# Two more token tiles transposed by DMA, the x loads re-ordered around it, and W1 loaded from two queues

## Chip, cores, metric

One core of one Trainium2 chip. The metric is the device time of one execution in microseconds (us); a time is the median of several runs, and a comparison uses runs of the two kernels taken on the same chip in the same rounds. Ratios are the mean time of one kernel's fast runs over that of the other's of the same rounds, so they are not quite the ratio of the medians quoted. "KB" is 1024 bytes.

## The reference

A layer norm of x (2048 tokens, 640 features) feeds two branches that are summed onto x: linear attention with 32 heads, and an MLP with GELU. Only the MLP's first product concerns us.

```python
xn = _layernorm(x)
h  = gelu(einsum("bsd,df->bsf", xn, w1) + b1)        # d = 640, f = 1536
return x + attention(xn, wqkv, wo) + einsum("bsf,fd->bsd", h, w2) + b2
```

## The kernel before

The 2048 tokens are 16 tiles of 128. Each is normalised token-major (`xn_tm`, DVE) and must be transposed (`xnT`) before TensorE (PE) can multiply it by W1. Tiles 0 to 3 are transposed by PE into PSUM and copied out; tiles 4 to 15 by a transposing DMA on the SP queue. A wait is placed by the helper `Pl.ins` from the `reads` and `writes` of each operation. The SP queue works in program order: a transposing DMA that waits for its tile also holds all that stands behind it. A "unit" below is 128 of W1's columns times one, two or four tiles: 5 products, one for each 128 of the 640 features. The code is shortened to its order:

```python
dma_x(0, 1)                                              # SP: x0
dma_w("scalar", W1[:, 0:KA, 0:FW], ..., r_W1A)           # ACT: 2/5 of W1's first third
dma_x(1, 1)
dma_w("sync", W1[:, KA:DT, 0:FW], ..., r_W1[0])          # SP: its other 3/5
dma_w1(1); dma_x(2, 1); dma_w1(2); dma_x(3, 1)           # W1's other thirds, whole; x2, x3
dma_x(4, 2); dma_x(6, 2); dma_x(8, 4); dma_x(12, 4)      # all other x, before any transpose
# ... [cut]
h_first(0, [0, 1, 2, 3], r_xnTA, ...)      # tiles 0, 1 with W1's first third, 128 columns
h_first(1, [0, 1, 2, 3], r_xnTA1)
units(0, 2, JQ, 2 * JQ + 1)                # tiles 0+1, 256 columns, 5 products a unit
ln_stats(2); ln_norm(2); ln_stats(3)
xnT_copy(2, transp(2))                     # PE transpose of tile 2, DVE copy
units(0, 2, 2 * JQ + 1, JT)
ln_next(3)                                 # statistics of tile 4 around the norm of 3
units(2, 1, 0, 3)
xnT_copy(3, transp(3))                     # the same for tile 3
units(2, 1, 3, 6); ln_next(4); units(3, 1, 0, 6); units(2, 2, 6, JT)
for t in range(TD, NT):                    # TD = 4
    if t > TD: ln_next(t)
    # SP: dma_start_transpose(xnT tile t <- xn_tm tile t)
```

Of the kernel before, what the change touches and what calls it, by code (L numbers as in the profile page):

```python
# [7 lines left out]
P = 128  # L8
# [104 lines left out]
def bass_parallel_sum__linear_attn_block__dense_activation_gelu__prompt_kernel(  # L113
# [4 lines left out]
    NT = S // P  # L118
    CH = 4
    CW = CH * P  # L120
    NC = NT // CH
    DT = D // P
    JT = F // P
# [6 lines left out]
    Pl = Planner(nc)  # L130
    R_ = Pl.res
# [5 lines left out]
    with contextlib.ExitStack() as es:  # L137
# [5 lines left out]
        xn_tm = sb("xn_tm", [P, NT, D], BF16)  # L143
        xnTf = sb("xnT", [P, DT * S], BF16)
        xnT = xnTf[:].rearrange("p (k s) -> p k s", k=DT)
# [4 lines left out]
        W1 = W1f[:].rearrange("p (k f) -> p k f", k=DT)  # L150
        GTb = W1f[:, 0:DT * D].rearrange("p (k d) -> p k d", k=DT)
        KVT = W1f[:, DT * D:2 * DT * D].rearrange("p (k d) -> p k d", k=DT)
# [27 lines left out]
        B_ = [R_("bank%d" % i) for i in range(8)]  # L180
# [10 lines left out]
        def bank(b, lo=0, hi=512):  # L191
            return ps[:, b * 512 + lo: b * 512 + hi]
# [10 lines left out]
        r_xn = [R_("xn%d" % t) for t in range(NT)]  # L203
        r_xnT = [R_("xnT%d" % t) for t in range(NT)]
        NW1 = 3
        r_W1A = R_("W1_0A")
        r_W1 = [R_("W1_%d" % i) for i in range(NW1)]
        r_Wq, r_Wk, r_Wv, r_W2, r_Wo = R_("Wq"), R_("Wk"), R_("Wv"), R_("W2"), R_("Wo")
        r_b1tmp, r_b1c, r_b2 = R_("b1tmp"), R_("b1c"), R_("b2")
# [8 lines left out]
        r_GT = [R_("GT%d" % f) for f in range(DT)]  # L218
        r_KVT = R_("KVT")
# [8 lines left out]
        def dma_x(t, n):  # L228
            src = xv[t * P:(t + n) * P, :].rearrange("(t p) d -> p t d", p=P)
            Pl.ins("sync", lambda e: e.dma_start(x_in[:, t:t + n, :], src),  # L230
                   writes=r_x[t:t + n], dma=True)

        def dma_w(eng, dst, src, res):
            Pl.ins(eng, lambda e: e.dma_start(dst, src), writes=[res], dma=True)

        w1v = B_w1.rearrange("(k p) n -> p k n", p=P)
        wqv = A_wqkv.rearrange("(k p) n -> p k n", p=P)
        FW = F // NW1
        def dma_w1(i, eng="sync"):
            dma_w(eng, W1[:, :, i * FW:(i + 1) * FW], w1v[:, :, i * FW:(i + 1) * FW], r_W1[i])  # L240
        KA = 2
        dma_x(0, 1)
        dma_w("scalar", b1tmp[:], B_b1.rearrange("(a p) -> a p", p=P), r_b1tmp)
        dma_w("scalar", W1[:, 0:KA, 0:FW], w1v[:, 0:KA, 0:FW], r_W1A)
        dma_x(1, 1)
        dma_w("sync", W1[:, KA:DT, 0:FW], w1v[:, KA:DT, 0:FW], r_W1[0])
        dma_w1(1)
        dma_x(2, 1)
        dma_w1(2)
        dma_x(3, 1)  # L250
        dma_x(4, 2)
        dma_x(6, 2)
        for c in range(2, NC):
            dma_x(c * CH, CH)
        x_done = len(Pl.records["sync"])
        dma_w("sync", Wqkv[:, :, D:2 * D], wqv[:, :, D:2 * D], r_Wk)
        dma_w("sync", Wqkv[:, :, 0:D], wqv[:, :, 0:D], r_Wq)
# [5 lines left out]
        g = "gpsimd"  # L263
# [8 lines left out]
               reads=[r_ident], writes=[r_ident])  # L272

        mask_jobs = []
# [15 lines left out]
        def run_masks(n):  # L290
            for _ in range(min(n, len(mask_jobs))):
                mask_jobs.pop(0)()


        def filler(n):
            b = take(1)
            Pl.ins("tensor", [lambda e: e.matmul(bank(b), warm[:, 0:P], warm[:], start=True, stop=True)
                              for _ in range(n)], reads=[r_warm], writes=[B_[b]])
# [25 lines left out]
        def ln_stats(t):  # L324
            ln_half(t, 0)
            ln_half(t, 1)
            ln_aggr(t)

        def ln_norm(t):
            s = t % 4  # L330
            Pl.ins(v, lambda e: e.tensor_scalar(xn_tm[:, t, :], x_in[:, t, :], aggr[:, s, 0:1], rstd[:, s:s + 1],
                                                ALU.subtract, ALU.mult),
                   reads=[r_x[t], r_aggr[s], r_rstd[s]], writes=[r_xn[t]])

        def transp(t):
            b = take(1)
            pT = bank(b).bitcast(BF16)[:, 0:D]
            Pl.ins("tensor", [(lambda e, k=k: e.transpose(pT[:, k * P:(k + 1) * P],  # L338
                                                          xn_tm[:, t, k * P:(k + 1) * P], ident[:]))
                              for k in range(DT)],  # L340
                   reads=[r_xn[t], r_ident], writes=[B_[b]])
            return b

        def xnT_copy(t, b):
            pT = bank(b).bitcast(BF16)[:, 0:D]
            Pl.ins(v, lambda e: e.tensor_copy(xnT[:, :, t * P:(t + 1) * P],
                                              pT.rearrange("p (k q) -> p k q", k=DT)),
                   reads=[B_[b]], writes=[r_xnT[t]])

        def h_unit(t0, n, jb):  # L350
            b = take(1)
            w = n * P
            tok = slice(t0 * P, t0 * P + w)
            Pl.ins("tensor", [(lambda e, k=k: e.matmul(  # L354
                bank(b, 0, w), W1[:, k, jb * P:(jb + 1) * P], xnT[:, k, tok],
                start=(k == 0), stop=(k == DT - 1))) for k in range(DT)],
                reads=[r_W1[jb * P // FW]] + r_xnT[t0:t0 + n], writes=[B_[b]])
            Pl.ins("scalar", lambda e: e.activation(  # L358
                HG[:, jb, tok], bank(b, 0, w), ACT.Gelu_apprx_tanh, bias=b1c[:, jb:jb + 1]),
                reads=[B_[b], r_b1c], writes=[r_HG[t][jb] for t in range(t0, t0 + n)])  # L360
# [20 lines left out]
        def h_first(t, jbs, resA, between=None):  # L381
            bs = [take(1) for _ in jbs]
            tok = slice(t * P, (t + 1) * P)
            for (ks, res) in (((0, 1), resA), ((2, 3, 4), r_xnT[t])):
                for i, (jb, b) in enumerate(zip(jbs, bs)):
                    Pl.ins("tensor", [(lambda e, k=k, jb=jb, b=b: e.matmul(  # L386
                        bank(b, 0, P), W1[:, k, jb * P:(jb + 1) * P], xnT[:, k, tok],
                        start=(k == 0), stop=(k == DT - 1))) for k in ks],
                        reads=[r_W1A if res is resA else r_W1[jb * P // FW], res], writes=[B_[b]])
                    if between and res is not resA and i in between:  # L390
                        between[i]()
            for jb, b in zip(jbs, bs):
                Pl.ins("scalar", lambda e, jb=jb, b=b: e.activation(
                    HG[:, jb, tok], bank(b, 0, P), ACT.Gelu_apprx_tanh, bias=b1c[:, jb:jb + 1]),
                    reads=[B_[b], r_b1c], writes=[r_HG[t][jb]])
# [2 lines left out]
        r_xnA1, r_xnB1 = R_("xn1A"), R_("xn1B")  # L398
        Pl.ins("scalar", lambda e: e.activation(b1c[:, 0:1], warm[:, 0:1], ACT.Gelu_apprx_tanh),
               reads=[r_warm], writes=[r_b1c])  # L400
        filler(6)
        b1_step()
        filler(3)
# [6 lines left out]
        dA, sA, bA = transp_part(0, 0, 2, r_xnA)  # L410
# [12 lines left out]
                                          3: lambda: copy_part(2, DT, r_xnB1, r_xnT[1])})  # L423
        h_first(1, [0, 1, 2, 3], r_xnTA1)

        TD = 4
        late = Pl.records["sync"][x_done:]
        del Pl.records["sync"][x_done:]
        JQ = JT // NW1

        def units(t0, n, lo, hi):
            for jb in range(lo, hi):
                h_unit(t0, n, jb)

        def ln_next(t):
            if t + 1 < NT:
                ln_half(t + 1, 0)
            ln_norm(t)
            if t + 1 < NT:
                ln_half(t + 1, 1)  # L440
                ln_aggr(t + 1)

        units(0, 2, JQ, 2 * JQ + 1)
        ln_stats(2)
        ln_norm(2)
        ln_stats(3)
        xnT_copy(2, transp(2))
        units(0, 2, 2 * JQ + 1, JT)
        ln_next(3)
        units(2, 1, 0, 3)  # L450
        xnT_copy(3, transp(3))
        units(2, 1, 3, 6)
        ln_next(4)
        units(3, 1, 0, 6)
        units(2, 2, 6, JT)
        for t in range(TD, NT):
            if t > TD:
                ln_next(t)
            Pl.ins("sync", lambda e, t=t: e.dma_start_transpose(xnT[:, :, t * P:(t + 1) * P], xn_tm[:, t, :]),
                   reads=[r_xn[t]], writes=[r_xnT[t]], dma=True)  # L460
        Pl.records["sync"] += late
        run_masks(len(mask_jobs))
        units(4, 1, 0, 3)
        units(5, 1, 0, 3)
        units(4, 2, 3, JT)
# [20 lines left out]
        for t in range(NT):  # L486
            b = take(2)
# [7 lines left out]
            phi(pair(b), b, 2, PK[:, t, :], r_PK[t], [r_x[t]])  # L495


        Pl.ins(g, lambda e: e.memset(KVT, 0.0), writes=[r_KVT] + r_W1)


        def z_step():
# [25 lines left out]
        for f in range(DT):  # L527
            b = take(2)
            for t in range(NT):
                Pl.ins("tensor", [(lambda e, t=t, h=h, b=b, f=f: e.matmul(  # L530
                    bank(b + h, 0, HW), xn_tm[:, t, f * P:(f + 1) * P],
                    PK[:, t, h * HW:(h + 1) * HW], start=(t == 0), stop=(t == NT - 1))) for h in range(2)],
                    reads=[r_xn[t], r_PK[t]], writes=B_[b:b + 2])
            Pl.ins("scalar", lambda e, b=b, f=f: e.activation(halves(GTb[:, f, :]), pair(b), ACT.Copy),  # L534
                   reads=B_[b:b + 2], writes=[r_GT[f]] + r_W1)


        def q_chunk(c):
# [154 lines left out]
        for t in range(4, NT - 1):  # L693
            b = out_w2(t)
# [47 lines left out]
```

## Time and profile before

| | before |
|---|---|
| median, 6 runs | 207.86 us (207.61 to 208.02) |
| span of the profile | 206.3 us |
| PE busy | 98% |
| PE waits between 6 and 60 us | none listed |
| first third of W1 complete | 6.19 us |
| PE's first product of the attention branch | 59.84 us |

The profile gives each engine's busy time, a chain of work followed back from the last instruction, and who waited for whom. PE is busy throughout, so the time moves only with PE's own work and waits. Everything before 59.84 us is the part that the change touches, everything after it is the same in both kernels.

### The profile page before, as it was taken

Reading aid. Unit: us, or ns where it says so; the run is one execution under the profiler, and the core shown is the slowest. Engines: PE = TensorE matmul, PEld = TensorE weight load, DVE = VectorE, ACT = ScalarE, POOL = GpSimd, SP = SyncE. Lnnn points to the kernel's source line nnn. Section 1 sums busy time; section 2 is a strip of 40 time slices with the busy share of each in tenths; the row PEclk is TensorE's granted clock in tenths of the full one; section 3 lists DMA queues with packets and bytes.
Section 4 is the critical chain, followed back from the end, with each engine's and each line's share of the span. In section 5 each row is a group of like instructions: output and inputs, shape, how many; then the busy total and the mean of one; then the engine's idle time right before and its main releaser. Section 6 shows DMA issues by size and latency. Waiting matters only on the chain.

```text
span 206.3 us, 3886 instructions
## 1 busy us (share of the span) xinstructions
PE 202.4 (98%) x1562; PEld 139.7 (68%) x1562; DVE 114.1 (55%) x233; ACT 72.5 (35%) x136; POOL 21.4 (10%) x59
## 2 busy tenths in 40 slices
PE   7999999999999999999999999999999999999996
PEld 2799987444457777777756556777777777777775
DVE  4677677100007888999298887574863422522332
ACT  3589887666676455111153553400000000000000
POOL 3243434730031000000000000000000000000000
DMA  6993445499900000000300001932112111000102
GB/s 187 359 344 68 76 90 93 86 366 323 340 7 0 0 0 3 0 0 3 64 0 5 0 0 29 379 105 52 71 56 60 62 38 52 35 32 32 37 32 65
DMA packets 23210, 18.31 MB, mean 89 GB/s; under 512 B 10392, under 2 KB 23192, under 8 KB 23192
## 3 DMA queue, kind: packets, MB, share of 16 engines
q1 hardware_dynamic: 22896, 17.80, 29.0%
q10 hardware_dynamic: 296, 0.27, 0.4%
q8 instruction: 12, 0.20, 0.4%
q14 instruction: 6, 0.05, 0.1%
HBM read 12.62 MB, written 2.62 MB: 74 GB/s over the span
## 4 chain that ended last, share of the span: by engine, by line
PE 96%; DVE 1%; DMA 1%; issue 0%; DVEq 0%
PE ps L633 34%; PE ps L354 24%; PE ps L530 11%; PE ps L491 11%; PE ps L542 10%; PE ps L669 2%; PE ps L569 1%; PE ps L386 1%; DMA xPK<-in_A_x_dram 1%; DVE stats L310 1%; PE ps L551 1%; PE ps L580 1%; PE ps L375 0%; PE ps L338 0%; DVE xn_tm L368 0%
## 5 line engine op out<-in xcount | busy, mean ns | idle before, releaser
L633 PE MATMUL ps<-W,HG 128*128 128x320 bf16 x360 | 51.0, 299 | 0.0
L354 PE MATMUL ps<-xnT,W 128*128 128x256 bf16 (+2 forms) x385 | 50.5, 293 | 0.0
L633 PEld LDWEIGHTS ps<-W,HG 128*128 128x128 bf16 x360 | 35.1, 98 | 14.2 <-issue 0.4
L354 PEld LDWEIGHTS ps<-xnT,W 128*128 128x128 bf16 x385 | 33.9, 98 | 15.9
L358 ACT ACTIVATE HG<-ps,b1c 128x256 bf16<-128x256 f32 (+2 forms) x77 | 38.0, 516 | 12.7 <-PE ps L354 10.3
L652 DVE TENSOR_TENSOR out_sb<-ps,xnT 128x640 bf16<-128x640 f32 x15 | 12.4, 825 | 35.0 <-PE ps L633 34.8
L478 ACT ACTIVATE ek<-ps 128x512 bf16<-128x512 f32 (+1 forms) x36 | 23.2, 645 | 20.3 <-PE ps L542 10.6
L479 DVE TENSOR_SCALAR ek<-ek 128x512 bf16<-128x512 bf16 (+1 forms) x36 | 10.9, 304 | 25.9 <-ACT ek L478 24.8
L633 PE MATMUL ps<-Msb,PQ 128*128 128x320 bf16 x150 | 22.3, 299 | 0.0
L542 PE MATMUL ps<-xnT,Wqkv 128*128 128x512 bf16 x100 | 21.9, 379 | 0.0
L491 PE MATMUL ps<-Wqkv,xnT 128*128 128x320 bf16 x160 | 21.9, 299 | 0.0
L530 PE MATMUL ps<-xPK,xn_tm 128*128 128x320 bf16 x160 | 21.9, 299 | 0.0
L491 PEld LDWEIGHTS ps<-Wqkv,xnT 128*128 128x128 bf16 x160 | 15.7, 98 | 6.2
L530 PEld LDWEIGHTS ps<-xPK,xn_tm 128*128 128x128 bf16 x160 | 15.7, 98 | 6.1
L633 PEld LDWEIGHTS ps<-Msb,PQ 128*128 128x128 bf16 x150 | 14.7, 98 | 5.7
L542 PEld LDWEIGHTS ps<-xnT,Wqkv 128*128 128x128 bf16 x100 | 11.7, 117 | 9.5
L310 DVE BATCH_NORM_STATS2 stats<-xPK 128x6 f32<-128x320 bf16 x32 | 14.7, 470 | 2.5 <-DMA xPK<-in_A_x_dram 2.5
L481 DVE SCALAR_TENSOR_TENSOR PQ<-ps,ek 128x512 bf16<-128x512 f32 x20 | 13.8, 692 | 2.1
L481 DVE SCALAR_TENSOR_TENSOR xPK<-ps,ek 128x640 bf16<-128x640 f32 x16 | 13.2, 824 | 1.7
L517 DVE TENSOR_TENSOR Msb<-Msb,xPK 128x640 f32<-128x640 f32 x14 | 11.6, 825 | 0.5
L320 POOL TENSOR_TENSOR rstd<-aggr,mhalf 128x1 f32<-128x1 f32 x16 | 9.1, 569 | 15.7 <-DVE aggr L318 15.7
L534 ACT ACTIVATE W<-ps 128x640 bf16<-128x640 f32 x5 | 3.5, 704 | 18.2 <-PE ps L530 18.2
(62 smaller groups left out, 98.2 us busy)
## 6 DMA issues: line engine op xcount, KB each, us to landing
xnT<-in_A_x_dram SPq DMA_DIRECT2D x4, 640.0 KB, 6.4
Wqkv<-in_A_wqkv_dram SPq DMA_DIRECT2D x3, 800.0 KB, 6.9
out_dram<-out_sb SPq DMA_DIRECT2D x15, 160.0 KB, 1.8
W<-in_B_w_dram SPq DMA_DIRECT2D x1, 1920.0 KB, 15.0
W<-in_B_w_dram SPq DMA_DIRECT2D x2, 640.0 KB, 6.7
xPK<-in_A_x_dram SPq DMA_DIRECT2D x2, 640.0 KB, 9.7
Wo<-in_A_wo_dram SPq DMA_DIRECT2D x1, 800.0 KB, 10.4
xPK<-in_A_x_dram SPq DMA_DIRECT2D x4, 160.0 KB, 4.4
```

The costliest lines, as they stand in the source:

```text
L310: Pl.ins(v, lambda e: e.bn_stats(stats[:, s, 6 * h:6 * h + 6], x_in[:, t, h * HW:(h + 1) * HW]), reads=[r_x[t]], writes=[r_stats[s][h]])
L354: Pl.ins("tensor", [(lambda e, k=k: e.matmul(bank(b, 0, w), W1[:, k, jb * P:(jb + 1) * P], xnT[:, k, tok], start=(k == 0), stop=(k == DT - ...
L358: Pl.ins("scalar", lambda e: e.activation(HG[:, jb, tok], bank(b, 0, w), ACT.Gelu_apprx_tanh, bias=b1c[:, jb:jb + 1]), reads=[B_[b], r_b1c ...
L478: Pl.ins("scalar", lambda e: e.activation(e2, src, ACT.Exp), reads=br, writes=[r_ek[s]])
L479: Pl.ins(v, lambda e: e.tensor_scalar(et, et, 1.0, 1e-6, ALU.min, ALU.add), reads=[r_ek[s]], writes=[r_ek[s]])
L481: Pl.ins(v, lambda e: e.scalar_tensor_tensor(out=d2, in0=src, scalar=0.0, in1=e2, op0=ALU.max, op1=ALU.add), reads=br + [r_ek[s]], writes= ...
L491: fns.append(lambda e, k=k, h=h, b=b, t=t: e.matmul(bank(b + h, 0, HW), xnT[:, k, t * P:(t + 1) * P], Wqkv[:, k, D + h * HW:D + (h + 1) * ...
L517: Pl.ins(v, lambda e, t=t: e.tensor_tensor(out=zsum, in0=zsum, in1=PK[:, t, :], op=ALU.add), reads=[r_PK[t], r_zsum], writes=[r_zsum])
L530: Pl.ins("tensor", [(lambda e, t=t, h=h, b=b, f=f: e.matmul(bank(b + h, 0, HW), xn_tm[:, t, f * P:(f + 1) * P], PK[:, t, h * HW:(h + 1) * ...
L542: Pl.ins("tensor", [(lambda e, k=k, j=j, b=b: e.matmul(bank(b), Wqkv[:, k, j:D:DT], xnT[:, k, cc], start=(k == 0), stop=(k == DT - 1))) fo ...
L633: return lambda e: e.matmul(bank(b + h, 0, HW), l, r[:, h * HW:(h + 1) * HW], start=(i == 0), stop=(i == JT + DT - 1))
L652: Pl.ins(v, lambda e: e.tensor_tensor(out=halves(out_sb[:, s, :]), in0=pair(b), in1=halves(x_res[:, t, :]), op=ALU.add), reads=B_[b:b + 2] ...
```

## The change

Intent: take 10 transposing products (and two DVE copies) from PE, the busiest engine, and give them to DMA engines that are idle most of the time. To make tiles 2 and 3 early enough, x2 and x3 are loaded ahead of W1's later thirds, W1's two later thirds are split over SP's and ACT's queue as the first already is, and x6 to x15 move behind the new transposes.

```diff
+        def dma_w1(i):    # SP: 3/5 of a third of W1
+            dma_w("sync", W1[:, KA:DT, i * FW:(i + 1) * FW], ..., r_W1[i])
+        def dma_w1a(i):   # ACT: the other 2/5
+            dma_w("scalar", W1[:, 0:KA, i * FW:(i + 1) * FW], ..., r_W1A[i])
         dma_x(1, 1)
-        dma_w("sync", W1[:, KA:DT, 0:FW], ...)
+        dma_w1(0)
+        dma_x(2, 1)
         dma_w1(1)
-        dma_x(2, 1)
+        dma_x(3, 1)
         dma_w1(2)
-        dma_x(3, 1)
         dma_x(4, 2)
-        dma_x(6, 2)
-        for c in range(2, NC):
-            dma_x(c * CH, CH)
...      # on ACT, just after its table load
+        dma_w1a(1)
+        dma_w1a(2)
...
-        [tiles 2 and 3: transp() and xnT_copy() between the units]
+        ln_stats(2)
+        for t in range(2, NT):
+            ln_next(t)
+            # SP: dma_start_transpose(xnT tile t <- xn_tm tile t)
+            if t == 3:
+                dma_x(6, 2)
+                dma_x(8, 4)
+            if t == 5:
+                dma_x(12, 4)
+        units(0, 2, JQ, JT)
+        units(2, 1, 0, 6)
         units(3, 1, 0, 6)
         units(2, 2, 6, JT)
```

More of the change, by code (lines that the diff above doesn't have):

```diff
@@ L205, in bass_parallel_sum__linear_attn_block__dense_activation_gelu__prompt_kernel @@
         NW1 = 3
-        r_W1A = R_("W1_0A")
+        r_W1A = [R_("W1_%dA" % i) for i in range(NW1)]
         r_W1 = [R_("W1_%d" % i) for i in range(NW1)]
@@ L238, in bass_parallel_sum__linear_attn_block__dense_activation_gelu__prompt_kernel @@
         FW = F // NW1
-        def dma_w1(i, eng="sync"):
-            dma_w(eng, W1[:, :, i * FW:(i + 1) * FW], w1v[:, :, i * FW:(i + 1) * FW], r_W1[i])
         KA = 2
+        def dma_w1(i):
+            dma_w("sync", W1[:, KA:DT, i * FW:(i + 1) * FW], w1v[:, KA:DT, i * FW:(i + 1) * FW], r_W1[i])
+        def dma_w1a(i):
+            dma_w("scalar", W1[:, 0:KA, i * FW:(i + 1) * FW], w1v[:, 0:KA, i * FW:(i + 1) * FW], r_W1A[i])
         dma_x(0, 1)
         dma_w("scalar", b1tmp[:], B_b1.rearrange("(a p) -> a p", p=P), r_b1tmp)
-        dma_w("scalar", W1[:, 0:KA, 0:FW], w1v[:, 0:KA, 0:FW], r_W1A)
+        dma_w1a(0)
         dma_x(1, 1)
-        dma_w("sync", W1[:, KA:DT, 0:FW], w1v[:, KA:DT, 0:FW], r_W1[0])
+        dma_w1(0)
+        dma_x(2, 1)
         dma_w1(1)
-        dma_x(2, 1)
+        dma_x(3, 1)
         dma_w1(2)
-        dma_x(3, 1)
         dma_x(4, 2)
-        dma_x(6, 2)
-        for c in range(2, NC):
-            dma_x(c * CH, CH)
         x_done = len(Pl.records["sync"])
@@ L356, in h_unit @@
                 start=(k == 0), stop=(k == DT - 1))) for k in range(DT)],
-                reads=[r_W1[jb * P // FW]] + r_xnT[t0:t0 + n], writes=[B_[b]])
+                reads=[r_W1A[jb * P // FW], r_W1[jb * P // FW]] + r_xnT[t0:t0 + n], writes=[B_[b]])
             Pl.ins("scalar", lambda e: e.activation(
@@ L388, in h_first @@
                         start=(k == 0), stop=(k == DT - 1))) for k in ks],
-                        reads=[r_W1A if res is resA else r_W1[jb * P // FW], res], writes=[B_[b]])
+                        reads=[r_W1A[jb * P // FW] if res is resA else r_W1[jb * P // FW], res], writes=[B_[b]])
                     if between and res is not resA and i in between:
@@ L424, in bass_parallel_sum__linear_attn_block__dense_activation_gelu__prompt_kernel @@
         h_first(1, [0, 1, 2, 3], r_xnTA1)
-        TD = 4
         late = Pl.records["sync"][x_done:]
@@ L441, in ln_next @@
                 ln_aggr(t + 1)
-        units(0, 2, JQ, 2 * JQ + 1)
         ln_stats(2)
-        ln_norm(2)
-        ln_stats(3)
-        xnT_copy(2, transp(2))
-        units(0, 2, 2 * JQ + 1, JT)
-        ln_next(3)
-        units(2, 1, 0, 3)
-        xnT_copy(3, transp(3))
-        units(2, 1, 3, 6)
-        ln_next(4)
+        for t in range(2, NT):
+            ln_next(t)
+            Pl.ins("sync", lambda e, t=t: e.dma_start_transpose(xnT[:, :, t * P:(t + 1) * P], xn_tm[:, t, :]),
+                   reads=[r_xn[t]], writes=[r_xnT[t]], dma=True)
+            if t == 3:
[3 more added lines that the diff above has]
+                dma_x(12, 4)
+        Pl.records["sync"] += late
+        run_masks(len(mask_jobs))
+        units(0, 2, JQ, JT)
+        units(2, 1, 0, 6)
         units(3, 1, 0, 6)
         units(2, 2, 6, JT)
-        for t in range(TD, NT):
-            if t > TD:
-                ln_next(t)
-            Pl.ins("sync", lambda e, t=t: e.dma_start_transpose(xnT[:, :, t * P:(t + 1) * P], xn_tm[:, t, :]),
-                   reads=[r_xn[t]], writes=[r_xnT[t]], dma=True)
-        Pl.records["sync"] += late
-        run_masks(len(mask_jobs))
         units(4, 1, 0, 3)
@@ L495, in bass_parallel_sum__linear_attn_block__dense_activation_gelu__prompt_kernel @@
             phi(pair(b), b, 2, PK[:, t, :], r_PK[t], [r_x[t]])
-        Pl.ins(g, lambda e: e.memset(KVT, 0.0), writes=[r_KVT] + r_W1)
+        Pl.ins(g, lambda e: e.memset(KVT, 0.0), writes=[r_KVT] + r_W1 + r_W1A)
         def z_step():
@@ L534, in bass_parallel_sum__linear_attn_block__dense_activation_gelu__prompt_kernel @@
             Pl.ins("scalar", lambda e, b=b, f=f: e.activation(halves(GTb[:, f, :]), pair(b), ACT.Copy),
-                   reads=B_[b:b + 2], writes=[r_GT[f]] + r_W1)
+                   reads=B_[b:b + 2], writes=[r_GT[f]] + r_W1 + r_W1A)
         def q_chunk(c):
```

## The prediction

> **What bounds the kernel now.** I read the busy table first, then the chain that ended last in order of time, then PE's waits after its start, then the timeline of DVE and of the SP queue, last the landings by tile.
>
> ```profile
> PE 202.4 (98%) x1562; PEld 139.7 (68%) x1562; DVE 114.1 (55%) x233; ACT 72.5 (35%) x136; POOL 21.4 (10%) x59
> ```
>
> PE is busy for 98% of a 206.3 us span, so only work or waits of PE can move the time. The early part of the chain (start us, us, what):
>
> ```profile
> 7.96 1.29 PE ps L386 x20
> 9.25 2.73 PE ps L354 x25
> 11.98 0.28 PE ps L338 x5
> 12.26 2.48 PE ps L354 x30
> 14.74 0.28 PE ps L338 x5
> 15.02 44.83 PE ps L354 x330
> ```
>
> Line 338 is the TensorE transpose of tiles 2 and 3, five 128x128 pieces each: 0.28 us apiece on the chain. From 9.25 us on the chain is PE alone, line after line. PE's waits from 4 us to 62 us are one, and that one is before 6 us:
>
> ```profile
> PE ps L375 <- DVE xn_tm L368: 0.7, 1, 0.7
> ```
>
> So tiles 2 and 3 and W1's later thirds reach PE in time today. How these arrive is in the timeline of DVE and SP (line 310 statistics, 331 normalisation, 459 the transposing DMA):
>
> ```profile
> 8.84 0.89 DVE L310 BATCH_NORM_STATS2 stats<-xPK 128x6 f32<-128x320 bf16 x2 [0.49 <-DMA xPK<-in_A_x_dram]
> 9.83 0.21 DVE L318 BATCH_NORM_AGGREGATE aggr<-stats 128x2 f32<-128x12 f32 x1
> 10.80 0.45 DVE L331 TENSOR_SCALAR xn_tm<-xPK,aggr,rstd 128x640 bf16<-128x640 bf16 x1 [0.76 <-POOL rstd L320]
> 13.12 0.45 DVE L331 TENSOR_SCALAR xn_tm<-xPK,aggr,rstd 128x640 bf16<-128x640 bf16 x1
> 16.32 3.12 SPq L459 DMA_TRANSPOSE xnT<-xn_tm  x2
> ```
>
> and for the twelve DMA transposes of today (issue ns, then issue to landing):
>
> ```profile
> L459 SPq DMA_TRANSPOSE xnT<-xn_tm x12: 1198/1200/1753, 16.3 to 37.9; - x12
> ...
> DMA to landing us min/median/max: 2.6/2.6/4.3
> ```
>
> A DMA transpose takes 1.2 us of the SP queue and lands 2.6 us after issue, sometimes 4.3. From start plus time to landing I get today's arrivals: W1's first 2/5 third (ACT queue) 1.45 + 4.2 = 5.65; its rest 6.2; W1's second third 2.24 + 6.1 = 8.35; x2 2.73 + 6.1 = 8.85; W1's last third 10.7; x3 11.1; x4-5 about 12.0. From 6 to 14 us the DMA row is at 9 tenths throughout, about 350 GB/s, that is 342 KB/us as the profile counts KB. The loads are bandwidth-bound here.
>
> **What the Trainium skill says.** (1) "VectorE: DVE Perf Modes", section "The three transpose paths", puts a 128x128 bf16 transpose at 390 ns on TensorE and 1309 ns by DMA. The trace agrees in direction: 0.28 us of PE's chain against 2.6 us of latency for a 128x640 tile, though the latency costs no engine anything if it is hidden. (2) "DMA: Bandwidth & Descriptors", section "Issuing engines are not separate DMA queues": the queues share the same 16 DMA engines and a second one only saves issue time. The trace agrees so far: two queues to 6 us, one after, both about 350 GB/s. So W1 on two queues adds no bandwidth; it changes the order of arrival. (3) Same page, "Queues, rings and completion order": an engine takes turns between queues packet by packet. I use it for an even split; today's trace has too little of both queues to test it. (4) "Runtime: NRT & Kernel Launch", section "Instruction fetch mechanics": instructions come in 16 KiB blocks by DMA. The trace shows 0.02 MB packets on q8 at 14.5-15, 22-22.5 and 34-34.5 us; the transposes issued at 20.2 and 32.1 us, whose data a fetch met, are the two that landed after 4.2 and 4.3 us.
>
> **The change part by part.**
> *Removed:* 10 PE transposes, 2 x 0.28 = 0.56 us off PE's chain, and two DVE copies of 0.49 us (off the chain). This is all that can be gained: 207.79 - 0.56 = 207.23.
> *W1 on two queues.* Up to 5.65 us the ACT queue is busy with the same data as before, then it goes on with 2 x 256 KB while SP still owes about 0.55 us x 342 = 188 KB of W1's first third. At half the rate (171 KB/us) this lands at 5.65 + 1.1 = 6.75. PE wants it after eight 128-column products (8 x 0.065 us) from 6.38, at 6.9: no wait, 0.15 us to spare. x2 lands at 6.75 + 160/171 = 7.7. ACT's 512 KB last until 5.65 + 512/171 = 8.65; SP has then 384 - 164 = 220 KB of W1's second third left, another 0.64 us: 9.3. Counted instead from today's 8.35 plus the 160 + 256 KB moved ahead of it (1.2 us) it is 9.55. PE wants it at 9.25: a wait of 0.05 to 0.3 us. x3 then lands near 10.05, W1's last third 11.2 (wanted at 9.3-9.55 + 20 x 0.109 = 11.5-11.7), x4-5 near 12.1: all bytes ahead of x4-5 are the same as before.
> *Tile 2.* DVE is free at 8.36, when x2 is there: statistics to 9.25, rstd by 10.25; but the first half of x3's statistics now stands ahead of the normalisation and waits for x3 (10.05). Normalised about 10.95, transpose issued at once, landed 10.95 + 2.65 = 13.6 or a little later, as x4-5 is ahead of it in the queue. PE first does 8 units of 5 x 0.109 = 4.36 us: 9.25 to 13.61, or to 13.9 after the W1 wait. Wait 0 to 0.2 us.
> *Tile 3.* Its normalisation stands behind statistics of x4 (12.1): 12.15 + 0.36 + 0.45 = 12.95; issue 13.0 (SP is free of the first transpose at 12.15); landed 15.65. PE finishes the six 128-column units of tile 2, 30 x 0.056 = 1.68 us, at 15.3 to 15.6. So PE waits till about 15.65 whatever happened before it: **tile 3's landing takes over from PE** for a moment.
> *Compared with today:* PE now starts tile 3's six units at 15.02 + 45 x 0.056 - 1.68 = 15.86. The change brings this to 15.65: 0.2 us gained, of 0.56 removed; 0.35 us goes into small waits. From there on PE's list is the same.
> *x6 on behind the transposes.* Issued at 14.2 and 14.65, landing about 17.0 (x6-7) and 18.8 (x8-11; 960 KB / 342 = 2.8 us). Tile 4's transpose sits behind these bytes in the queue and lands about 19.5-20; PE wants it at 15.65 + 1.68 + 30 x 0.109 = 20.6. Tile 5: x6's statistics 17.05, normalised 17.9, landed 20.55; wanted at 21.4. Both hidden, by under 1 us. x12-15 then goes out near 19-20.5, tiles 6 and 7 land before 25.7, wanted at 27. Later tiles follow DVE's pace of 1.92 us, unchanged.
> *Sum:* 207.79 - 0.56 + 0.35 = **207.6 us**.
>
> **Rivals.**
> *A, the full gain:* every new wait is hidden, 207.2. For it: tile 2 and W1 miss by 0.2 to 0.3 us at most in my sums. Against it: tile 3 hangs on x4-5, whose bytes are not fewer than before.
> *B, a late transpose:* one lands after 4.2 us in place of 2.6. For it: PE's instruction block fetched today at 14.5-15 belongs to about its 60th product from 9.25; in the new order that is 40 x 0.109 + 20 x 0.056 us on, at 14.75-15.05, 1.8-2.05 us after tile 3's issue. The two slow ones of today met their fetch 1.8 to 2.4 us after issue. Against it: half a microsecond either way avoids it. If it happens, tile 3 lands at 17.2 and PE waits 1.5 us more: 209.1. I give this 3 in 10.
> *C, loads win:* ACT's two W1 pieces take more than half the engines, W1's first third comes after 6.9 and its second after 9.6, or x6-11 pushes tile 4 beyond 20.6: 208.0 to 208.8.
> *D, ACT's issues* (0.4 us each in its own queue) hold up its copy of tile 0 at 5.85: they should end by 2.7, or by 4.1 if they wait for the table load that ends at 3.17. Nothing.
>
> **Range and chances.** The middle is the sum above, the low end lies just under A, the high end just over B: 207.0 to 209.2. Two per cent is 4.2 us. The gain is capped at 0.56 us, and it takes three late transposes at once to lose 4.2: faster 0.005, within 2% 0.98, slower 0.015.
>
> **What would show it.** Right: no line 338 on the chain; PE busy down by some 0.5 to 1 us; one or two PE waits of under 0.4 us, for a W1 load near 9.3-9.6 and for a DMA into xnT near 13.6 and 15.6; line 354 alone from 16 to 60 us; everything after it as long as before (60 us to the end). Wrong: a PE wait of over 1 us at tile 3 with a landing of 4 us (B); a wait near 7, 9.3 or 20.6 us with the loads late (C); PE with no wait at all (A). The step I trust least is the 2.65 us to landing of the two new transposes, as they run beside loads.

## The result, and the profile after

The changed kernel took **210.19 us** (median of 6 runs, 208.81 to 211.44) against 207.86: ratio 1.0115, 95% interval 1.0075 to 1.0155. It is within 2%, as forecast, but above the stated range (207.0 to 209.2), and instead of a small gain it is a loss of 2.3 us. Its runs spread over 2.6 us, those of the kernel before over 0.4 us.

Line numbers shift by two: 356 is the old 354, 388 the old 386, 377 the old 375. The page of the profiled run (211.44 us), its busy row and the granted PE clock in tenths over 40 slices:

```profile
PE 204.5 (97%) x1552; PEld 140.8 (67%) x1552; DVE 113.4 (54%) x231; ACT 72.8 (35%) x136; POOL 21.3 (10%) x59
...
PEclk9979999999999999999999999999999999999999
```

Ten products are gone, yet busy time has risen by 2.1 us. The seven in the clock row says why. The stretches of the windows view (columns: us; busy us and count of PE, PEld, DVE, ACT, POOL; PEclk; DMA share; GB/s):

```profile
6.70:10.10 3.40, 1.58 (x26) 1.35 (x25) 1.18 (x4) 0.46 (x2) 0.31 (x1) 1.00 1.06 360
10.10:13.50 3.40, 3.40 (x31) 3.10 (x28) 2.54 (x8) 2.01 (x7) 0.99 (x3) 0.50 0.27 95
13.50:16.90 3.40, 3.40 (x33) 3.04 (x31) 2.39 (x8) 2.82 (x6) 1.53 (x4) 1.00 0.48 77
```

In the first stretch PE was busy for 1.58 of 3.4 us; in the next the clock was 0.50, then full again. The idle time is in PE's waits and in the chain (start us, us, what):

```profile
PE ps L388 <- DMA W<-in_B_w_dram: 1.8, 1, 1.8
...
PE ps L377 <- DVE xn_tm L370: 0.4, 1, 0.4
```

```profile
1.73 7.49 DMA W<-in_B_w_dram
9.21 0.05 issue
9.26 0.51 PE ps L388 x6
...
13.27 4.29 DMA xnT<-xn_tm
17.56 0.04 issue
17.61 45.84 PE ps L356 x345
```

W1's first third, issued at 1.73, was complete at 9.21 us (6.19 before, 6.75 forecast), and tile 2's transpose, issued at 13.27, landed after 4.29 us (2.65 forecast). Only this one of the six runs (211.44 us) had a stretch at half clock (mean clock 0.992); the other five took 208.81 to 210.86 at full clock. So I profiled the same kernel once more (last experiment), in a run at full clock; the accounting below uses that one.

### The profile page after: what moved, and what is told of

It reads as the page before. It is cut to its first block, busy times and chain, and to the rows that moved or that the text cites. A ratio compares the mean times of both kernels' runs of the same rounds, so it can differ in the third digit from the quotient of the medians.

```text
span 209.9 us, 3868 instructions
## 1 busy us (share of the span) xinstructions
PE 204.5 (97%) x1552; PEld 140.8 (67%) x1552; DVE 113.4 (54%) x231; ACT 72.8 (35%) x136; POOL 21.3 (10%) x59
## 4 chain that ended last, share of the span: by engine, by line
PE 91%; DMA 6%; DVE 1%; SPq 0%; POOL 0%; issue 0%; DVEq 0%
PE ps L632 33%; PE ps L356 22%; PE ps L529 10%; PE ps L490 10%; PE ps L541 10%; DMA W<-in_B_w_dram 4%; PE ps L668 2%; DMA xnT<-xn_tm 2%; PE ps L568 1%; PE ps L550 1%; PE ps L579 1%; PE ps L388 0%; DVE stats L312 0%; SPq L230 0%; POOL rstd L322 0%
```

## The experiments

**Theories.** *Q*: the second queue makes the slowest of the 16 DMA engines late with W1, and PE waits. *T*: the DMA transposes land too late for PE, whatever W1 does; its parts are *F* (a transpose whose data meets an instruction fetch lands late) and *B* (x6 to x15, now between the transposes, hold the transposes behind them). *X*: x2 and x3 ahead of W1 starve PE. All times in the table below are medians of 5 or 6 runs except e14's (4 runs); "before" is the kernel before in the same rounds. The ratios leave out runs: one of e1 (216.21 us), one of e9 (213.6) and one of the kernel before, beside e5 to e8 (358.72, clock 0.562).

| run | time | before | ratio (95%) | PE waits listed, 6 to 62 us |
|---|---|---|---|---|
| e1 one queue | 209.56 | 207.80 | 1.0079 (1.0066-1.0092) | tile 2 1.5, 29 us 0.4 (slow run) |
| e2 two queues alone | 208.72 | 207.80 | 1.0054 (1.0019-1.0089) | W1 0.5 |
| e3 transposes alone | 209.55 | 207.80 | 1.0091 (1.0068-1.0114) | tile 2 1.0, 29 us 1.3, DVE 0.6 |
| e4 ACT pieces later | 211.12 | 207.80 | 1.0137 (1.0107-1.0167) | W1 2.1 |
| e5 fetch moved | 209.48 | 208.07 | 1.0073 (1.0053-1.0092) | tiles 3, 4 1.9, W1 0.3 |
| e6 x12 later | 208.78 | 208.07 | 1.0039 (1.0024-1.0053) | tile 2 1.3, tile 11 0.4 |
| e7 both | 210.27 | 208.07 | 1.0109 (1.0090-1.0127) | tile 5 1.1, tile 11 0.8 (listed under ACT), ACT 0.2 |
| e8 control | 207.97 | 208.07 | 1.0002 (0.9989-1.0015) | none |
| e9 tile 3 alone | 210.77 | 208.08 | 1.0138 (1.0112-1.0164) | tiles 4, 5 2.1 |
| e10 one ACT piece | 208.82 | 208.08 | 1.0043 (1.0022-1.0063) | W1 0.3 |
| e11 x in pairs | 208.74 | 207.90 | 1.0032 (1.0015-1.0048) | tile 3 0.5, W1 0.4 |
| e12 all remedies | 208.41 | 207.90 | 1.0031 (0.9999-1.0064) | tiles 3, 11 0.7 |
| e13 pieces on SP | 209.31 | 208.05 | 1.0074 (1.0054-1.0095) | tile 2 1.4, 29 us 0.3 |
| e14 after again | 210.69 | 208.05 | 1.0134 (1.0115-1.0153) | W1 0.2, tile 2 1.0, 29 us 0.5, others 0.7 |

### W1 on two queues: e2, e4, e10, e13

**e2** is the kernel before with nothing changed but W1's three thirds split over the two queues.

```diff
-        dma_w1(1)   # whole, SP        (same for 2)
+        dma_w1(1)   # 3/5, SP
...      # on ACT, just after its table load
+        dma_w1a(1)  # 2/5, ACT         (same for 2)
```

> The kernel before with one thing changed: W1's three thirds each 2/5 on ACT's queue and 3/5 on SP's. Tiles 2 and 3 still transposed by PE, loads in the old order. Theory Q: W1's first third on SP lands at 7.5 to 9.5 us instead of 6.2, PE waits 0.7 to 2 us before 10 us, 208.8 to 211 with runs spread over 1 us or more. Theories T and X: as the kernel before, 207.8, spread 0.4 us.

Measured 208.72 us, spread 3.0 us; one run had the half clock (210.87). Chain of its profile:

```profile
1.73 5.81 DMA W<-in_B_w_dram
7.53 0.05 issue
7.58 0.51 PE ps L391 x6
```

So two queues alone cost 0.5% and most of the spread, a little below what I wrote for Q (208.8 to 211); T and X are excluded as the whole cause.

**e13** issues the same pieces at the same place of the order, but all on SP's queue: does the queue matter, or only the bytes close behind W1's first third?

```diff
         dma_w1(0)
+        dma_w1a(1)      # on SP
         dma_x(2, 1)
+        dma_w1a(2)      # on SP
         dma_w1(1)
```

> The changed kernel with W1's two later 2/5 pieces issued at the same place of the order (behind W1's first third and behind x2) but on SP's queue. If the second queue is what makes the slowest engines late, W1's first third lands at 5.7 to 6.7 us, no PE wait there, and the time is that of e1 (209.2 to 209.8; tile 2 late, tiles 6 and 7 late). If it is the early bytes, it lands at 7.5 us or later in one queue too, and 210 or more.

The first third was complete at 6.03 us, PE did not wait for it, and the time is e1's. The trace has 16 completion counts for each of these DMAs; I read them as one for each of the 16 engines. Their times, in order, for SP's part of W1's first third:

```
us           1st    8th    14th   15th   16th
before       5.20   5.60   5.87   5.88   6.19
e13, SP      5.26   5.48   5.71   5.78   6.03
e4, ACT late 5.14   5.45   5.65   5.66   5.67
after        5.33   5.79   6.79   7.61   9.21
e14 (after)  5.38   5.73   6.87   7.18   7.44
e2           5.34   5.74   7.30   7.45   7.53
e10          5.11   5.96   6.82   7.18   7.29
```

With ACT's later pieces in a second queue at the same time, the 8th engine is 0.3 to 0.5 us later than in e13, but the 14th is 1.1 to 1.6 us later and the last 1.3 to 3.2, and PE needs all 16. My step took the two queues to share evenly on every engine. On average they nearly did: between 5.7 and 7.5 us SP and ACT moved 0.28 and 0.29 MB (after), 0.27 and 0.30 (e14), 0.39 and 0.26 (e2). But the middle of the 16 was earlier than the 6.75 us of an even split, and the end far later. The gap is wider than the scatter between profiles: the eleven profiles with no later piece on ACT's queue have the last count at 5.96 to 6.82 us (e3 is the latest), the four with one or two from the start at 7.29 to 9.21. Why single engines fall behind, the trace does not tell (it names no engine); this stays open.

**e10** puts one of the two later pieces on ACT.

```diff
         dma_w1a(1)
-        dma_w1a(2)      # the last third whole on SP
```

> As e2_two_queues_alone, with only one of the two later W1 pieces on ACT's queue (the last third whole on SP). If ACT's early bytes delay the slowest engines of W1's first third in proportion, it lands at 6.6 to 7.2 us (e2: 7.5, before: 6.2), PE waits 0 to 0.4 us, 207.7 to 208.6, spread under 1 us. If any second piece brings the whole delay, 7.5 us or later and 208.7.

7.29 us and 1.0043: not told apart from e2 by time. In these two profiles the delay is not in proportion to ACT's bytes: most of it (1.10 of 1.34 us over the kernel before) is there with one piece.

**e4** is the changed kernel with ACT's pieces issued after its copy of tile 0, at 6.27 us instead of 1.96.

```diff
-        dma_w1a(1)
-        dma_w1a(2)
...      # after ACT's copy of tile 0
+        dma_w1a(1, [r_xnTA])
+        dma_w1a(2)
```

> The changed kernel, but ACT issues its two later W1 pieces only after its copy of tile 0 (about 6.3 us instead of 2 us), so W1's first third has the engines to itself and ACT's first piece. Theory Q in the form of competition with the first third: it lands at about 6.2 us, no PE wait at 7 us, but the later thirds may then be late: PE wait under 1 us near 9.3 to 11 us; 207.5 to 209. Theory Q in the form that any second queue delays single engines: later thirds with a last engine 1 us or more behind the 14th, a wait at 9.3 us of over 1 us. Theory T: 208.8 or more with a wait for xnT.

Neither form of Q foresaw what came. The first third is complete at 5.67 us, as Q says, but W1's second third (ACT's part) only at 11.28, and PE waits for that:

```profile
PE ps L357 <- DMA W<-in_B_w_dram: 2.1, 1, 2.1
```

All SP loads issued before 6.27 us, x4-5 too (10.63), were complete before that ACT piece: a later start in an empty queue gave it no turn ahead of them. Four of e4's six runs had the half clock: 211.05 to 211.39 us, the other two 209.60 and 209.85. So it costs about 1.5 us here. In e14, though, a run with mean clock 0.992 took 210.75 us amid 210.26 to 210.90 of the others: no cost to be seen. In the two profiles that show the half clock it follows a PE wait of 1.8 and 2.1 us; but the profiled run of e9 had a wait of 1.9 us at full clock. That such a wait brings it on is therefore not shown.

### The transposes: e1, e3, e5, e6, e7, e8

**e1** is the changed kernel without the second queue.

```diff
-            dma_w("sync", W1[:, KA:DT, ...])
+            k0 = KA if i == 0 else 0
+            dma_w("sync", W1[:, k0:DT, ...])
...
-        dma_w1a(1)
-        dma_w1a(2)
```

> The changed kernel with W1's second and last third whole on the SP queue again; x2, x3 ahead of them, tiles 2 and 3 by DMA, x6 on behind. Theory Q (W1's two pieces on ACT's queue make the last DMA engines of W1's first third late, PE waits 1.8 us for it): the first third lands at 6.2 us as in the kernel before, no PE wait at 7-9 us, full clock, 207.2 to 208.0. Theory T (the DMA transposes land too late for PE, here after 4.3 us): the PE wait for xnT stays, 208.8 or more. Theory X (x2 and x3 ahead of W1's later thirds starve PE): a PE wait for W1 at 9.3 us or later.

The first third is there at 6.04 us, without a PE wait, and the runs lie within 0.5 us, apart from the profiled one, which fell in the slow state (216.21 us, clock 0.95) and is not compared by time. The early waits do not hang on that run: e13's fast run has the same ones (1.4 and 0.3 us). The fast runs are still at 1.0079: theory T. With e2's 0.54% this makes 1.33%, against 1.15% and 1.34% measured for the whole change, so the two parts about add up, and the larger one is the transposes'. Tile 2's transpose in the tile view:

```profile
L448 SPq DMA_TRANSPOSE xnT<-xn_tm x1: 1316/1316/1316, 11.1 to 11.1; - x1
DMA to landing us min/median/max: 4.5/4.5/4.5
```

**e3** is the kernel before with only the transposes of tiles 2 and 3 given to DMA (and x6 on behind them).

```diff
         [as e1, and:]
-        dma_x(2, 1)
         dma_w1(1)
-        dma_x(3, 1)
+        dma_x(2, 1)
         dma_w1(2)
+        dma_x(3, 1)
```

> The kernel before with tiles 2 and 3 transposed by DMA and x6 on behind these transposes; W1 on SP as before, x2 and x3 behind W1's second and last third as before. Theory Q: no wait before 10 us; x2 lands at 8.8, tile 2 lands about 14, so a PE wait of 0 to 0.5 us there; 207.2 to 208.2. Theory T: PE waits over 1 us at tile 2 or 3, 208.8 or more.

209.55 us: theory T, and not told apart from e1. Moving x2 and x3 forward made no net difference, so X falls as a main cause. A small part of it is real: W1's second third, complete at 8.33 us before, is complete at 9.33 in e1 and at 9.54 and 9.56 in e5 and e11, where PE waits 0.3 and 0.4 us for it. In e3 tile 2's transpose was issued at 12.39 (x2 and x3 came later) and landed in 2.75 us. The chain shows a second wait further on:

```profile
15.18 13.79 PE ps L357 x165
28.98 1.34 issue
30.32 32.61 PE ps L357 x180
```

The 165 products reach from tile 2 to the end of tiles 4 and 5; the next unit wants tiles 6 and 7. Tile 7's transpose, issued at 24.27, landed at 30.22, behind x12-15 (landed 26.67) and tile 6 (28.84). The view writes "issue" here, though the landing fits to 0.1 us.

**e6** moves x12-15 from behind tile 5's transpose to behind tile 8's.

```diff
-            if t == 5:
+            if t == 8:
                 dma_x(12, 4)
```

> As e1_one_queue, with x12-15 issued after tile 8's transpose instead of after tile 5's. Theory B (640 KB of x12-15 ahead of tiles 6 and 7 in the queue make these land at 28 to 30 us, PE waits 0.4 to 1.3 us at 29): tiles 6 and 7 land by 27, that PE wait is gone, 208.8 to 209.3 as tile 2's wait stays. If the fetch alone makes tiles 6 and 7 late, the wait stays.

Against e1 the ratio falls from 1.0079 to 1.0039, the wait at 29 us is gone, and what remains is at tile 2 (1.3 us) and at tile 11 (0.4 us):

```profile
11.09 4.32 DMA xnT<-xn_tm
15.40 0.05 issue
15.45 19.94 PE ps L357 x225
35.38 0.44 issue
```

Tiles 6 and 7 landed at 23.44 and 27.44, so B is shown. Tile 7 was late in e6 too (issued 22.81, 4.6 us), so one late transpose alone is not enough for the wait at 29 us. The net gain is about 0.4% (e1 and e6 ran on different chips, each beside the kernel before). Tile 11 is the price: its transpose now follows x12-15 (landed 31.90), was issued at 32.79 and landed at 35.36.

**e5** leaves e1 as it is and cuts nine warm-up products of 512 columns at the start into 36 of 128, so that PE's first 16 KB instruction block is fetched earlier: 27 products more, so the block is used up sooner.

```diff
-        filler(6)
+        filler(24, P)
...
-        filler(3)
+        filler(12, P)
```

> As e1_one_queue, with PE's nine warm-up products of 512 columns at the start cut into 36 of 128 columns: 27 more products, so PE's first 16 KB instruction block, met at 13.0 us by tile 2's transpose in e1, should be fetched 2 to 3 us earlier, before that transpose is issued. Theory F (a DMA transpose whose data meets an instruction fetch lands 1.5 to 2 us late): tile 2 lands 2.6 to 3 us after issue instead of 4.5, PE's wait for it falls from 1.5 us to under 0.5; the wait at tiles 6 and 7 may stay or grow; 208.2 to 209.3. Theory L (it is late because it stands behind loads in the queue): 4 us or more again.

The block was fetched at 10.85 us instead of 13.04, and tile 2's transpose, issued at 10.88 us, landed in the usual time:

```profile
L448 SPq DMA_TRANSPOSE xnT<-xn_tm x1: 1527/1527/1527, 10.9 to 10.9; - x1
DMA to landing us min/median/max: 2.7/2.7/2.7
```

Across the runs, tile 2's issue, the start of that fetch after it, and the time to landing:

```
            issue us   fetch after   landed after
e3          12.39      -0.27         2.75
e12         11.01      -0.39         2.72
e5          10.88      -0.03         2.74
e7          10.75      +0.47         3.18
e14 (after) 11.55      +1.10         4.22
e1          11.07      +1.97         4.49
after       13.27      +1.97         4.29
e13         10.85      +2.20         4.27   (15 of 16 engines 2.67)
e6          11.09      +2.29         4.32   (15 of 16 engines 2.77)
e11         10.91      +2.42         2.73
e4          10.70      +2.68         2.70
```

In this table a fetch that starts 1.1 to 2.3 us after the transpose's issue costs it about 1.6 us; one up to 0.5 us after it, before it, or 2.4 us and more after it costs 0 to 0.5 us. The transposes of all 16 traces together bear this out, if those with a load or a late transpose still ahead of them are left out: all 18 with a fetch 1.1 to 2.2 us after their issue landed after 4.1 to 4.8 us, all 10 with one 2.6 to 4.0 us after it landed after 2.6 to 2.7 us; at 2.2 to 2.4 us, and in the first microsecond, it went either way. F is shown for tile 2 by e5 against e1. Whether it strikes is partly luck: up to tile 2, e1, e6 and e11 are the same program, and e11's tile 2 was not delayed. But the time of e5 (1.0073) is that of e1: the next block, 9.7 us later, now met tile 4's transpose, which stood behind x6-11, landed at 22.82 and made PE wait 1.3 us.

**e8** is the control: the same small warm-up products in the kernel before.

> Control: the kernel before with the same 36 small warm-up products. If cutting them costs PE nothing, 207.6 to 208.0. If the warm-up suffers (half clock later, or tile 0's transposes wait for PE), 208.3 or more, and e5 and e7 have to be read against this one.

1.0002: the cut costs nothing. A fetch met tile 4's transpose here too (issued 16.33, landed at 20.58, 4.25 us), without any PE wait, because PE wants that tile at about 20.8 (15.86 + 1.68 + 3.27, by the prediction's sums). The kernel before has late transposes as well; it has the slack for them.

**e7** joins e5 and e6.

> e5 and e6 together. If F and B are the two costs of the DMA transposes, PE waits under 0.6 us in all from 4 to 62 us and the time is at or below the kernel before: 207.2 to 207.9. If something else costs the rest, 208.5 or more.

A miss: 1.0109, worse than either. Tile 2 was in time (13.93), but the fetch at 20.65 met tile 5 (issued 18.65, landed 22.90) and PE waited 1.1 us. A further 0.8 us, which the view puts down to ACT, was tile 11's: issued at 31.49 and met by the next fetch (33.46), it landed at 35.77, and PE's next product began at 36.23, 0.46 us later, just as in e6 (35.36 and 35.82).

### Slack: e9, e11, e12

**e9**: e6 with tile 2 on PE again, and PE doing all units of tile 2 before tile 3's.

```diff
...      [the rest of tile 2's path to PE as in the kernel before]
+        xnT_copy(2, transp(2))
-        units(2, 1, 0, 6)
-        units(3, 1, 0, 6)
-        units(2, 2, 6, JT)
+        units(2, 1, 0, JT)
+        units(3, 1, 0, JT)
```

> As e6_x12_later (W1 on one queue, x12-15 after tile 8's transpose), but tile 2 is transposed by PE again and PE does all twelve 128-column units of tile 2 before it wants tile 3 (about 17.2 us instead of 15.4). Theory S (what decides is the slack between a transpose's landing and PE's want): tile 3 issued about 13.6 lands at 16.3, or at 18 if a fetch meets it; PE waits 0 to 0.7 us instead of 1.8; 207.5 to 208.3. If the loads behind the transposes cost PE something by themselves, 208.6 or more.

A miss in time (210.77 us, 207.5 to 208.3 expected), half a miss in mechanism. Two of its six runs had a mean clock of 0.992 (211.88 us, and the slow 213.6). Tile 3 landed at 16.60 with no PE wait, as S says, but tile 4 (issued 16.35, behind x6-11, which landed at 20.74, and met by the fetch at 20.61) landed at 22.75, and PE waited 1.9 us for it:

```profile
22.80 1.01 PE L357 MATMUL ps<-xnT,W 128*128 128x128 bf16 x15 [1.90 <-DMA xnT<-xn_tm]
```

**e11** is e1 with x6 to x15 loaded in pairs, spread between the transposes.

```diff
-            if t == 3:
-                dma_x(6, 2)
-                dma_x(8, 4)
-            if t == 5:
-                dma_x(12, 4)
+            if t in (3, 4, 5, 7, 9):
+                dma_x({3: 6, 4: 8, 5: 10, 7: 12, 9: 14}[t], 2)
```

> As e1_one_queue, with x6 to x15 loaded in pairs between the transposes: x6-7 after tile 3's, x8-9 after 4's, x10-11 after 5's, x12-13 after 7's, x14-15 after 9's, so that no transpose has more than 320 KB ahead of it. Theory B: tiles 4 to 7 land before PE wants them (tile 4 by 19, tile 5 by 21, tiles 6 and 7 by 27), no PE wait but the one at tiles 2 and 3 (1.3 us, a fetch meets tile 2): 208.3 to 208.9, at or a little below e6 (208.8). If these waits stay, 209.3 or more.

1.0032. Tiles 4 to 7 landed at 18.94, 21.77, 26.02 and 26.72 and PE waited for none of them; its waits are 0.5 us for tile 3 and 0.4 us for W1. The wait of 1.3 us that I expected at tile 2 did not come, by the luck of the fetch (2.42 us after the issue), so the gain over e1 is not the pairs' alone.

**e12** adds the earlier fetch and normalises tiles 2 and 3 before the statistics of the next tile.

```diff
-        filler(6)
+        filler(24, P)
-        filler(3)
+        filler(18, 80)
...
+            if t < 4:
+                ln_norm(t)
+                ln_stats(t + 1)
+            else:
                 ln_next(t)
```

> e11 with two more remedies: the warm-up cut into 42 small products, so that PE's instruction block is fetched at about 10 us, before tile 2's transpose is issued; and tiles 2 and 3 normalised before the statistics of the next tile, so that they need not wait for x3 and x4-5. If fetch, queue and order are all that cost the DMA transposes, tile 2 lands by 13.5, tile 3 by 15.6, PE waits under 0.5 us in all and the time is 207.2 to 207.8, at or below the kernel before. If a fetch meets a transpose that PE waits for all the same, 208.3 or more.

A miss (207.2 to 207.8 expected). Its 1.0031 (0.9999 to 1.0064) is the lowest ratio of the versions that transpose tiles 2 and 3 by DMA, though not told apart from e11's: not told apart from the kernel before either, and not better. PE's listed waits are down to 0.7 us, but a third fetch (32.09 us) met tile 11 (landed 34.58) and PE waited 0.3 us for it. In the profile the attention branch still begins 1.04 us later than before: 0.32 by PE's first 256-column product (9.41 for 9.09), 0.67 by these waits, less the 0.56; some 0.6 us are not assigned. So e12 does not show that fetch, queue and order are all that the DMA transposes cost. No version tried beats the kernel before.

**e14** is the changed kernel again, for a profile at full clock.

> The changed kernel again, unchanged. W1's first third lands between 7.0 and 9.5 us and PE waits 0.3 to 2 us for it; if the clock stays full, the profiled run takes 208.8 to 210.9, as five of its six runs did.

The profiled run took 210.26 us, inside the spread of the first six; its wait for W1's first third was 0.2 us, a little under what I expected. Its PE timeline and chain:

```profile
7.49 0.51 PE L388 MATMUL ps<-xnT,W 128*128 128x128 bf16 x6 [0.19 <-DMA W<-in_B_w_dram]
...
10.29 4.53 PE L356 MATMUL ps<-xnT,W 128*128 128x256 bf16 x40 [0.38 <-issue]
...
15.81 13.39 PE L356 MATMUL ps<-xnT,W 128*128 128x128 bf16 x165 [1.00 <-DMA xnT<-xn_tm]
```

```profile
11.55 4.22 DMA xnT<-xn_tm
15.77 0.05 issue
15.81 13.39 PE ps L356 x165
29.20 0.46 issue
29.66 6.71 PE ps L356 x60
```

The attention branch begins at 62.27 us instead of 59.84: 2.43 us later. In order: PE's first 256-column product starts at 10.29 instead of 9.09, which is 1.20 (x1's last engine at 4.61 instead of 4.05, W1's first third at 7.44, its second at 10.20; x1 was as late in e3, 4.86, with one queue, so not all of this is shown to come from the second queue); the wait for tile 2 is 1.00; the wait at tiles 6 and 7 is 0.46; the transposes removed are worth -0.56. The sum is 2.10; 0.3 us are not assigned.

## Why the prediction was wrong, point by point

- **What is removed, 0.56 us: as forecast.** Ten products are gone, and line 338 is off the chain (the 0.56 us is read from the kernel before, not measured by itself). It was also rightly named as the most that could be gained.
- **"At half the rate this lands at 6.75 ... no wait, 0.15 us to spare": the first step that failed.** It landed at 9.21 and 7.44 us in the two profiles. The even split was a mean over 16 engines; a DMA is complete with its slowest. By e13 it is the second queue that does this, not the bytes; by e2 it costs 0.54%. Rival C named the late W1 and gave 208.0 to 208.8 for it, but for another reason, more than half the rate for ACT; the bytes were near half and half (0.27 and 0.30 MB in e14), so that reason was not it.
- **W1's second third, "a wait of 0.05 to 0.3 us":** complete at 11.29 (after) and 10.20 (e14) instead of 9.3 to 9.55; PE idle 0.38 us in e14.
- **Tile 2, "landed 10.95 + 2.65": failed, and with the later tiles it is the larger loss (0.79% by e1).** In e14 the transpose was issued at 11.55, 0.6 us late with x3 (10.66 instead of 10.05), and landed after 4.2 us, 1.6 late; in the first profile after 4.3. The mechanism was rival B's, but I let it hit tile 3 at 3 in 10. In the profiles the fetches of this stage come 6 to 15 us apart and the transposes about 2 us apart over some 28 us, so some transpose was all but sure to be met; which one, and whether it had slack, decided. The fetch came also earlier than I worked out (12.65 us in e14). The prediction also counted two late transposes in the kernel before; its trace has a third, issued at 34.03, just behind the second, and landed after 3.7 us.
- **"Tile 3's landing takes over from PE": did not come about**, because tile 2's did, at 15.77 to 17.56 us.
- **"Tiles 6 and 7 land before 25.7 ... hidden": failed.** They landed at 28.27 and 29.57 us in e14. The terms were too small: x12-15 went out at 21.30 (19 to 20.5 forecast) and needed 4.9 us to land, at 26.17, where the sums for x8-11, as many bytes, give 4.15 (14.65 to 18.8); and a fetch at 26.16 met tile 6. By e1 against e6 this costs 0.4% when PE is otherwise early.
- **Tile 4 at 19.5 to 20, tile 5 at 20.55:** 21.77 and 22.65 in e14, and hidden there only because PE was already late. In e5 and e9, where PE was earlier, tile 4 became the wait.
- **Not foreseen at all:** the half clock after a wait of 1.8 us: about 1.5 us in this kernel's first runs and in e4, nothing to be seen in e14's one run with it.
- **Range and chances:** the cap on the gain and the low chance of a 2% loss held. The high end was rival B alone; B, C and the lateness of tiles 6 and 7 came together, and they do not exclude one another.

## What to carry to other kernels

Taking work from the busiest engine gains at most that work (here 0.56 us), and pays only if what replaces it has slack: compare the landing, with its slow case, to the time at which the engine wants it, tile by tile. A transfer is as late as the slowest of its 16 engines, so do not work out a landing from the mean rate alone; here a second queue, opened beside a load that was about to be waited for, made the last engine 1.3 to 3.2 us later though the bytes were shared near evenly. Loads that used to run ahead of a chain of transposes delay it when they are moved in between.

## What the Trainium skill lacked or had wrong

- "DMA: Bandwidth & Descriptors", "Issuing engines are not separate DMA queues", says that a second issuing engine only saves issue time. Here it also made the last engine of the load in the other queue 1.3 to 3.2 us later (7.3 to 9.2 us, against 6.0 with the same pieces in the same order on one queue), at a cost of 0.5% by itself.
- The same page, "Queues, rings and completion order", has the engines take turns between queues packet by packet. A 256 KB piece issued at 6.27 us on ACT's empty queue was complete at 11.28, after all that SP had issued before it (10.63): by completions nearer to order of issue than to turns. With both queues full from the start the bytes were near even (0.27 and 0.30 MB, e14, 5.7 to 7.5 us). The trace does not show why.
- "Runtime: NRT & Kernel Launch", "Instruction fetch mechanics", calls the cost of crossing a 16 KiB boundary mostly hidden. It is not for a DMA transpose in flight: a block fetched 1.1 to 2.3 us after the issue of a DMA transpose made it land after 4.2 to 4.5 us instead of 2.7 (tile 2; much the same in 18 transposes of all traces). I found no page that has this.
- "TensorE: Matmul & The Clock Gate", "HAM oscillation", gives idle gaps above about 3.4 us as what to avoid. Here PE idle for 1.8 us, in a stretch of 3.4 us with 1.58 us busy, was followed by 3.4 us at clock 0.50, and so was a wait of 2.1 us in e4; a wait of 1.9 us in e9 was not.
- No page that I found gives the time of a transposing DMA from SBUF to SBUF of 128x640 bf16: 1.2 us of the issuing queue and 2.6 us to landing.
